# GpSimd's low parts wait for VectorE's: a scheduling hint becomes a dependency in an attention and channel-mixing kernel

## The chip, the cores and the metric

The kernel runs on one NeuronCore of a Trainium2 chip. The metric is the device time of one launch in microseconds. A core has five engines that run their own instruction queues in order and wait for one another by semaphores: TensorE (PE, with its weight loads shown apart as PEld), VectorE (DVE), ScalarE (ACT), GpSimd (POOL) and SyncE (SP), which here only issues DMA transfers.

## The reference

Eight batches, eight heads, 576 tokens, head size 64. First a windowed attention with a linear bias per head, then a mixing block on the attention's output:

```
scores = (q @ k^T) / sqrt(64) + slope[h] * -|i - j|, masked to 0 <= i - j < 128
x      = softmax(scores) @ v                    # [B, 576, 512], heads side by side
theta  = x @ w_theta
y      = w_tok_r @ (x * cos(theta)) + w_tok_i @ (x * sin(theta))
u      = x + y
out    = u + max(u @ w_ch, 0)
```

All inputs and outputs are float32.

## The kernel before

Products that need float32 accuracy are made of two parts. An operand is rounded to a high part, and the rest, operand minus high part, is its low part; a product is high x high + high x low + low x high. ACT makes the high parts (`qh`, `kh`, `vh`, `u_hi`, `z_hi`), and DVE or GpSimd the low parts: `ql` (L311) and `vl` (L331) on DVE, `kl` (L315) and `u_lo` (L573) on GpSimd, `z_lo` (L463) on either.

The work goes batch by batch. A batch of attention has four **pair steps**, g = 0 to 3, each for two heads; here g = 0 is the first step of a batch. In a step (`attend`) PE transposes the probabilities of the current pair (`flip`, into `t_ps`; ACT and DVE copy them out as the two parts of `pt`, L410 and L411), computes the scores of the next pair in three lots (the first into an `mm` bank, the others into `s_ps`; DVE adds the bias and takes the minimum at L395, ACT exponentiates at L398 into `last` and `s_sb`), and multiplies probabilities by values (`values`, into `acc`); DVE divides by the row sums (`finish`, L446 to L449, into `x_sb`). Between these pieces PE does the token mixing of the batch before (`mix`, products of `wtk` and `z`); at its end `u` is formed (DVE, L569), rounded (ACT, `u_hi`, L571) and its low part collected in a list, `lows`, that the step emits at its end. Then comes the **turn**: `x` is transposed, theta, cosine and sine are computed and `z` is made for the next batch's token mixing, with the channel mixing (`channels`, the products with `wch`) of the batch before in between.

Operands are prepared ahead. `prepare`, called in the middle of a step behind the first head's division, splits the q and k of one pair (`split_pair`: `qh`, `ql`, `kh`, `kl`) and then issues the loads of the next one: three transfers into `qr`, one into `kr` (L211 to L215), on SP's queue, which also carries the value loads (`vb`) and the outputs. `qr` and `kr` are single buffers: the next load waits until `qh` and `ql`, or `kh` and `kl`, have been made. The pair that is split in step g has its scores computed in step g + 1.

A scheduler lays down each engine's queue from the program's dependencies, from priorities and from hints. PE's order is pinned to the program's. A block under `tc.issue_after(ins)` puts an ordering edge, without a semaphore, from each instruction of the block that stands on the engine of `ins` to `ins`; an instruction of another engine gets none by it. The hints around `kl` and around `lows` name a DVE instruction (`ql`, or the second head's `vl`), while `kl` and `u_lo` are GpSimd's.

Of the kernel before, what the change touches and what calls it, by code (L numbers as in the profile page):

```python
# [11 lines left out]
F32 = mybir.dt.float32  # L12
# [6 lines left out]
ALU = mybir.AluOpType  # L19
# [27 lines left out]
def attn_moe_kernel(ctx: ExitStack, tc: tile.TileContext, qt, kt, vx, wth, wtok, wch, band, out):  # L47
    nc = tc.nc
# [19 lines left out]
    pinned, lows = [], []  # L68

    def mm(*args, **kw):  # L70
        ins = nc.tensor.matmul(*args, **kw)  # L71
        if pinned:
            tc.keep_in_program_order(ins)

    def flipped(*args):
        ins = nc.tensor.transpose(*args)  # L76
        if pinned:
            tc.keep_in_program_order(ins)
# [153 lines left out]
    def measure(g):  # L232

        vb = group_v[g]
        peak = peaks[g % 2]
        most = peak[:, :GROUP]
        nc.vector.tensor_reduce(out=most, in_=vb[:, :, :, :64], axis=mybir.AxisListType.XY, op=ALU.max,
                                apply_absolute_value=True)  # L240
        nc.vector.tensor_scalar(out=most, in0=most, scalar1=2.0 ** -100, scalar2=None, op0=ALU.max)
        group_v[g] = vb, peak
# [13 lines left out]
    def spread_to(diag, n, part):  # L256
        w_ps = ps_m.tile([128, 512], F32, name="mm")
        mm(w_ps[:, :n], ones.broadcast_to([128, 128]), diag, start=True, stop=True)
        scale = rings["scale" + part].take()
        power(scale, w_ps[:, :n], VEXP)  # L260
        return scale
# [12 lines left out]
    def spread_first(g):  # L274
        vb, peak = group_v[g]
        group_v[g] = vb, spread_from(peak, GROUP, "")

    def spread_scales(g):
        vb, diag = group_v[g]
        scale = spread_to(diag, GROUP, "")  # L280
        group_v[g] = vb, scale
        if g % 2:
            c = rings["scale"].at + (g // 2 - 1) % 2 * 2 * GROUP
            batch_scale(g // 2, fixed[:, c:c + 2 * GROUP])
# [19 lines left out]
    def split_pair(p, raw):  # L304

        qr, kr = raw
        qh, ql = (qk.tile([128, S + 64], F32R, name=name) for name in ("qh", "ql"))
        kh, kl = (qk.tile([128, S], F32R, name=name) for name in ("kh", "kl"))
        sc = scales[:, p % (H // 2):p % (H // 2) + 1]
        nc.scalar.activation(qh, qr, AF.Copy, scale=sc)  # L310
        low = nc.vector.scalar_tensor_tensor(out=ql, in0=qr, scalar=sc, in1=qh.bitcast(F32), op0=ALU.mult,  # L311
                                             op1=ALU.subtract)
        nc.scalar.copy(kh, kr)  # L313
        with tc.issue_after(low.ins) if pinned else nullcontext():
            nc.gpsimd.tensor_tensor(out=kl, in0=kr, in1=kh.bitcast(F32), op=ALU.subtract)  # L315
        return (qh, kh), (ql, kh), (qh, kl)

    def split_values(n):
# [27 lines left out]
    class Pair:  # L346
# [12 lines left out]
        def scores(self, tiles, behind=None):  # L359

            last = len(self.terms) - 1
            if tiles == (0,):
                _, _, k0, kn, _ = TILES[0]
                ps = ps_m.tile([128, 512], F32, name="mm")
                for j, (qm, km) in enumerate(self.terms):
                    mm(ps[:, :kn], qm[:, 512:], km[:, k0:k0 + kn], start=(j == 0), stop=(j == last))
                whole = lasts[self.p % len(lasts)]
                self.weigh(0, 0, whole[:, :kn], ps[:, :kn], bands[:, 512:], behind)
                self.sc[0, 0] = whole
                return  # L370
# [175 lines left out]
    def mix(st):  # L546

        xtf, z_hi, z_lo = st["xtf"], st["z_hi"], st["z_lo"]
        u_hi = big.tile([128, 4, S], F32R, name="u_hi")
        u_lo = big.tile([128, 4, S], F32R, name="u_lo")  # L550
        st.update(u_hi=u_hi, u_lo=u_lo)
        banks = {}
        seq = (8, 0, 4, 1, 5, 2, 6, 3, 7)

        def part(g, ks):
            hf, m = divmod(g, 4)
            cs = slice(hf * HALF, hf * HALF + HALF)
            if g not in banks:
                banks[g] = ps_m.tile([128, 512], F32, name="mm")
            y_ps = banks[g]  # L560
            for k in ks:
                c = seq[k]
                for n, (z, w) in enumerate(((z_hi, wtk_hi), (z_hi, wtk_lo), (z_lo, wtk_hi))):
                    mm(y_ps[:, :HALF], z[:, c, m * 128:m * 128 + 128], w[:, c, cs],
                       start=(k == 0 and n == 0), stop=(k == 8 and n == 2))
                if k < 8:
                    yield
            if ks[-1] == 8:
                nc.vector.scalar_tensor_tensor(out=xtf[:, m, cs], in0=y_ps[:, :HALF], scalar=st["back"],  # L569
                                               in1=xtf[:, m, cs], op0=ALU.mult, op1=ALU.add)  # L570
                nc.scalar.copy(u_hi[:, m, cs], xtf[:, m, cs])  # L571
                def low(m=m, cs=cs):
                    nc.gpsimd.tensor_tensor(out=u_lo[:, m, cs], in0=xtf[:, m, cs], in1=u_hi[:, m, cs].bitcast(F32),  # L573
                                            op=ALU.subtract)

                if st["b"] + 1 < B:
                    lows.append(low)
                else:
                    low()
                yield  # L580

        begun = 2 if st["b"] + 1 < B else 3
        for ks in (range(7), range(7, 9)):
            for g in range(begun):
                yield from part(g, ks)
        for g in range(begun, 8):
            yield from part(g, range(9))
# [28 lines left out]
    def prepare(p):  # L616

        if 0 <= p - 1 < pairs and p - 1 not in parts:
            parts[p - 1] = split_pair(p - 1, raw.pop(p - 1))
        if p < pairs and p not in raw:  # L620
            raw[p] = load_pair(p)

    def step(stream, k=1):
        for _ in range(k):
            next(stream, None)

    def attend(b, x_sb, mixing, chans, first, behind):

        for g in range(H // 2):
            p = b * H // 2 + g  # L630
            pair = first.pop(0)
            one, two = pair.heads
            new = None
            if p + DEPTH < pairs:
                new = Pair(p + DEPTH)
                first.append(new)
            measured = p // 2 + 1 if p % 2 == 0 and p + 2 < pairs else None
            scaled = p // 2 + 1 if p % 2 and p + 1 < pairs else None

            def scores(tiles):  # L640
                if new is not None:
                    new.scores(tiles, behind)

            steps = STEPS[min(g, 2)]
            pair.flip(0)
            pair.flip(2)
            step(mixing, steps[0])
            scores(SCORES[0])
            scores(SCORES[1])
            step(mixing, steps[1])  # L650
            pair.flip(1)
            pair.flip(3)
            step(mixing, steps[2])
            if scaled:
                with tc.high_priority(FINISH):
                    spread_first(scaled)
            one.values()
            with tc.high_priority(FINISH):
                done = one.finish(x_sb)
            scores(SCORES[2])  # L660
            if scaled:
                with tc.high_priority(FINISH):
                    spread_scales(scaled)
            with tc.issue_after(done.ins):
                if new is not None:
                    new.heads[0].ready()
                prepare(p + DEPTH + 2)
            step(mixing, steps[3])
            if g >= 2:
                step(chans)  # L670
            two.values()
            with tc.high_priority(FINISH):
                done = two.finish(x_sb)
            if new is not None:
                with tc.issue_after(done.ins):
                    done = new.heads[1].ready()
                    with tc.issue_after(done.ins):
                        for low in lows:
                            low()
                    if measured:  # L680
                        measure(measured)
            else:
                for low in lows:
                    low()
            lows.clear()
# [142 lines left out]
```

## Time and profile before

| | us |
|---|---|
| median of three runs | 732.91 (732.55 to 734.18) |
| profiled execution | 731.11, span 729.2 |
| busy: PE / DVE / ACT / POOL | 678.5 / 556.5 / 500.2 / 155.9 |
| `kl` L315, x32, busy, mean of one | 55.4, 1.73 |
| `u_lo` L573, x64, busy, mean of one | 50.6, 0.80 |

The busy times overlap, and each is counted over the whole span. Times in the profile's rows count from the start of the span. A row of the timeline gives start, duration, engine, line, operation, tiles (written, then read), shapes and, in brackets, how long the engine had been idle before and what ended that. The first 125 us or so are the start, in which weights are unpacked and the first batch's attention is computed; from there to about 640 us the same batch of four pair steps and a turn repeats, and the rest is the last batch's mixing.

### The profile page before, as it was taken

What the parts mean: (1) busy time and instruction counts of PE and PEld (TensorE: products, weight loads), DVE (VectorE), ACT (ScalarE), POOL (GpSimd) and SP (SyncE); (2) the same over time, 40 slices, a digit from 0 to 9 for tenths busy, and PEclk for the clock granted to TensorE, in tenths of its full rate; (3) what the DMA queues carried; (4) which work ended last, traced back from release to release, by engine and by line L of the source; (5) the groups of instructions that cost most, each with busy time, mean ns of one, the idle gap of its engine ahead of it and who ended that gap; (6) DMA issues with size and microseconds to landing.
All of it is one profiled execution on the core that took longest, in us unless ns stands there. A gap on an engine that the chain in (4) does not pass through costs nothing.

```text
span 729.2 us, 16045 instructions
## 1 busy us (share of the span) xinstructions
PE 678.5 (93%) x6219; PEld 578.7 (79%) x6221; DVE 556.5 (76%) x1528; ACT 500.2 (69%) x988; POOL 155.9 (21%) x200
## 2 busy tenths in 40 slices
PE   3889887999999999899999999899989999899998
PEld 2558765889878888788877898789878898789787
DVE  6988956887688967987688967987788967974722
ACT  4888467676966678666966678666966678654810
POOL 2211302321212302321212302321212301210220
PEclk9885588999999999999999999999999999999999
DMA  9556110232012310232012310232012310000001
GB/s 306 162 180 203 43 40 1 71 82 88 25 36 77 101 52 18 71 105 68 26 33 75 97 56 18 79 99 71 24 41 65 101 50 18 18 10 33 26 9 58
DMA packets 32620, 49.86 MB, mean 68 GB/s; under 512 B 5664, under 2 KB 22048, under 8 KB 32544
## 3 DMA queue, kind: packets, MB, share of 16 engines
q1 hardware_dynamic: 32544, 48.84, 21.9%
q8 instruction: 49, 0.80, 0.4%
q14 instruction: 27, 0.22, 0.1%
HBM read 39.39 MB, written 9.44 MB: 67 GB/s over the span
## 4 chain that ended last, share of the span: by engine, by line
PE 44%; DVE 25%; ACT 23%; issue 3%; DMA 3%; SPq 1%; POOL 0%; ACTq 0%; DVEq 0%; POOLq 0%
PE mm L71 28%; PE acc L71 6%; PE t_ps L76 5%; PE s_ps L71 4%; DVE pt L411 4%; ACT g L511 3%; ACT z_hi L462 3%; ACT g L510 3%; DVE ql L311 2%; ACT xtf L484 2%; DVE s_sb L395 2%; DVE g L515 2%; ACT x_hi L482 2%; DVE f L515 2%; ACT s_sb L398 1%
## 5 line engine op out<-in xcount | busy, mean ns | idle before, releaser
L71 PE MATMUL mm<-wtk_hi,z_lo 128*128 128x288 f16 x576 | 165.3, 287 | 5.6 <-DVE z_lo L463 5.0
L71 PE MATMUL mm<-wtk_hi,z_hi 128*128 128x288 f16 x576 | 165.7, 288 | 3.9 <-ACT z_hi L462 3.9
L71 PE MATMUL mm<-wtk_lo,z_hi 128*128 128x288 f16 x576 | 165.2, 287 | 0.0
L398 ACT ACTIVATE s_sb<-s_sb,fixed 128x256 f32<-128x256 f32 (+1 forms) x256 | 105.0, 472 | 50.4 <-DVE fixed L395 50.3
L71 PEld LDWEIGHTS <-z_hi 128*128 128x128 f16 x1152 | 109.1, 99 | 33.5 <-ACT z_hi L462 4.4
L573 POOL TENSOR_TENSOR u_lo<-xtf,u_hi 128x288 fp32r<-128x288 f32 x64 | 50.6, 797 | 293.1 <-ACT u_hi L571 277.6
L411 DVE SCALAR_TENSOR_TENSOR pt<-t_ps,pt 128x512 f16<-128x512 f32 x112 | 75.5, 686 | 37.3 <-ACT pt L410 36.9
L395 DVE CUSTOM_DVE_ANT_0 s_sb<-s_ps,bands 128x256 f32<-128x256 f32 (+1 forms) x256 | 85.5, 383 | 1.2 <-PE s_ps L71 1.2
L71 PEld LDWEIGHTS <-z_lo 128*128 128x128 f16 x576 | 56.4, 98 | 24.2 <-DVE z_lo L463 9.2
L76 PE MATMUL t_ps<-fixed,s_sb 128*128 128x128 f32 x448 | 66.0, 282 | 10.1 <-DVE pt L411 5.6
L315 POOL TENSOR_TENSOR kl<-kr,kh 128x576 fp32r<-128x576 f32 x32 | 55.4, 1731 | 63.6 <-ACT kh L313 63.6
L76 PEld LDWEIGHTS t_ps<-fixed,s_sb 128*128 128x128 f32 x448 | 51.9, 145 | 16.9 <-DVE pt L411 6.8
L410 ACT ACTIVATE pt<-t_ps 128x512 f16<-128x512 f32 x112 | 62.1, 580 | 4.1 <-PE t_ps L76 4.1
L571 ACT CAST u_hi<-xtf 128x288 fp32r<-128x288 f32 x64 | 27.1, 425 | 43.1 <-DVE xtf L569 43.1
L71 PE MATMUL acc<-vh,pt 128*128 128x65 f16 x1008 | 55.6, 194 | 0.0
L71 PEld LDWEIGHTS <-pt 128*128 128x128 f16 x1512 | 52.6, 98 | 2.7
L463 POOL TENSOR_TENSOR z_lo<-g,z_hi 128x512 f16<-128x512 f32 x16 | 19.2, 1198 | 160.4 <-ACT z_hi L462 160.4
L71 PE MATMUL acc<-vl,pt 128*128 128x64 f16 x504 | 52.1, 193 | 0.0
L71 PE MATMUL s_ps<-kh,qh 64*128 64x256 f32 (+1 forms) x256 | 44.2, 342 | 7.4 <-DVE fixed L395 7.3
L71 PE MATMUL mm<-wth_hi,x_hi 128*128 128x512 f32 x160 | 47.7, 421 | 3.2 <-ACT x_hi L482 1.7
L71 PE MATMUL mm<-u_hi,wch_hi 128*128 128x288 f32 x256 | 47.2, 306 | 0.0
L569 DVE SCALAR_TENSOR_TENSOR xtf<-mm,fixed,xtf 128x288 f32<-128x288 f32 x64 | 32.2, 512 | 18.7 <-PE mm L71 18.6
(141 smaller groups left out, 1540.9 us busy)
## 6 DMA issues: line engine op xcount, KB each, us to landing
vb<-in_vx_dram SPq DMA_DIRECT2D x16, 650.0 KB, 5.3
kr<-in_kt_dram SPq DMA_DIRECT2D x32, 288.0 KB, 3.2
out_dram<-xtf SPq DMA_DIRECT2D x64, 144.0 KB, 1.8
qr<-in_qt_dram SPq DMA_DIRECT2D x32, 144.0 KB, 2.7
qr<-in_qt_dram SPq DMA_DIRECT2D x32, 128.0 KB, 2.7
xtf<-in_wtok_dram SPq DMA_DIRECT2D x4, 576.0 KB, 4.6
u_hi<-in_wtok_dram SPq DMA_DIRECT2D x3, 576.0 KB, 4.6
u_lo<-in_wtok_dram SPq DMA_DIRECT2D x2, 576.0 KB, 5.9
```

The costliest lines, as they stand in the source:

```text
L71: ins = nc.tensor.matmul(*args, **kw)
L76: ins = nc.tensor.transpose(*args)
L315: nc.gpsimd.tensor_tensor(out=kl, in0=kr, in1=kh.bitcast(F32), op=ALU.subtract)
L395: nc.vector.tensor_tensor_reduce(out=sb, in0=ps, in1=bias, scale=2.0 ** -(2 * self.p % H + 1), scalar=3.0e38, op0=ALU.add, op1=ALU.min, ac ...
L398: self.exp = nc.scalar.activation(sb, sb, AF.Exp, bias=least, scale=-1.0)
L410: nc.scalar.activation(pt[:, 0], t_ps, AF.Copy, scale=2.0 ** PEXP)
L411: nc.vector.scalar_tensor_tensor(out=pt[:, 1], in0=t_ps, scalar=2.0 ** PEXP, in1=pt[:, 0], op0=ALU.mult, op1=ALU.subtract)
L462: st["turned"] = nc.scalar.copy(z_hi[:, c, :], z)
L515: nc.vector.scalar_tensor_tensor(out=z, in0=x_sb[:, i, :], scalar=zs[:, c:c + 1], in1=z, op0=ALU.mult, op1=ALU.mult)
L569: nc.vector.scalar_tensor_tensor(out=xtf[:, m, cs], in0=y_ps[:, :HALF], scalar=st["back"], in1=xtf[:, m, cs], op0=ALU.mult, op1=ALU.add)
L571: nc.scalar.copy(u_hi[:, m, cs], xtf[:, m, cs])
L573: nc.gpsimd.tensor_tensor(out=u_lo[:, m, cs], in0=xtf[:, m, cs], in1=u_hi[:, m, cs].bitcast(F32), op=ALU.subtract)
```

## The change

`kl` is made to wait, by a semaphore, for `ql` of the same pair, and each collected `u_lo` for the second head's `vl` of the step (`new.heads[1].ready()` returns it). A helper adds the dependency; the hints go. `kl` before the pinned part, and `u_lo` of the last batch, stay as they were.

```diff
+    def after(what, done):
+        tc.add_manual_dep(what.ins, done.ins.name, mybir.DependencyInfo(mybir.DependencyClass.Sync,
+                                                                         mybir.DependencyReason.DATA))
...
         nc.scalar.copy(kh, kr)
-        with tc.issue_after(low.ins) if pinned else nullcontext():
-            nc.gpsimd.tensor_tensor(out=kl, in0=kr, in1=kh.bitcast(F32), op=ALU.subtract)
+        rest = nc.gpsimd.tensor_tensor(out=kl, in0=kr, in1=kh.bitcast(F32), op=ALU.subtract)
+        if pinned:
+            after(rest, low)
...
                 def low(m=m, cs=cs):
-                    nc.gpsimd.tensor_tensor(out=u_lo[:, m, cs], in0=xtf[:, m, cs], in1=u_hi[:, m, cs].bitcast(F32),
-                                            op=ALU.subtract)
+                    return nc.gpsimd.tensor_tensor(out=u_lo[:, m, cs], in0=xtf[:, m, cs],
+                                                   in1=u_hi[:, m, cs].bitcast(F32), op=ALU.subtract)
...
                 with tc.issue_after(done.ins):
                     done = new.heads[1].ready()
-                    with tc.issue_after(done.ins):
-                        for low in lows:
-                            low()
+                    for low in lows:
+                        after(low(), done)
```

The scheduler then lays the queues down anew. The orders of PE and DVE stay the same, row by row. GpSimd's queue in the first two pair steps of a batch (the one whose `ql` stands at 212.76 us in the profile) was this before. Numbers behind a tile's name tell buffers apart: `kl_2821` belongs to the pair whose `qh` is `qh_2818`, and `kl_2581` to the pair ahead of it; in brackets stand the engines or DMA queues whose semaphores are waited for.

```order
L573 TENSOR_TENSOR u_lo_2406<-xtf_2120,u_hi_2405 128x288 [waits Activation_49,Pool_49]
L573 TENSOR_TENSOR u_lo_2406<-xtf_2120,u_hi_2405 128x288 [waits Activation_49]
L330 MEMSET vh_2573 128x5 [waits PE_49]
L315 TENSOR_TENSOR kl_2821<-kr_2589,kh_2820 128x576 [waits DMAHW5_49,PE_49,Activation_49]
L330 MEMSET vh_2631 128x5 [waits PE_49,Pool_49]
L573 TENSOR_TENSOR u_lo_2406<-xtf_2120,u_hi_2405 128x288 [waits Activation_49]
L330 MEMSET vh_2813 128x5 [waits PE_49,Pool_49]
L573 TENSOR_TENSOR u_lo_2406<-xtf_2120,u_hi_2405 128x288 [waits Activation_49]
L315 TENSOR_TENSOR kl_3047<-kr_2829,kh_3046 128x576 [waits DMAHW0_49,PE_49,Activation_49]
```

And now (its line numbers are those of the changed kernel, four or five higher):

```order
L335 MEMSET vh_2573 128x5 [waits PE_49,Pool_49]
L318 TENSOR_TENSOR kl_2581<-kr_2054,kh_2580 128x576 [waits DMAHW4_49,DVE_49]
L335 MEMSET vh_2631 128x5 [waits PE_49,Pool_49]
L578 TENSOR_TENSOR u_lo_2406<-xtf_2120,u_hi_2405 128x288 [waits DVE_49,Pool_49]
L578 TENSOR_TENSOR u_lo_2406<-xtf_2120,u_hi_2405 128x288 [waits Activation_49]
L335 MEMSET vh_2813 128x5 [waits PE_49,Activation_49,Pool_49]
L318 TENSOR_TENSOR kl_2821<-kr_2589,kh_2820 128x576 [waits DMAHW7_49,DVE_49,Activation_49]
```

Each `kl` stands one pair step later, with a wait for DVE, and two `u_lo` stand together at the end of each step, the first of them with a wait for DVE. ACT's queue changes with it, from the first head's `vh` of that step to the exponentials of the next scores. Before:

```order
L329 ACTIVATE vh_2573<-vb_1387,fixed_103 128x5x64 [waits PE_49]
L313 CAST kh_2820<-kr_2589 128x576 [waits DMAHW5_49,PE_49]
L398 ACTIVATE s_sb512_2551<-s_sb512_2551,fixed_103 128x256 [waits DVE_49]
...
L410 ACTIVATE pt_2655<-t_ps_2650 128x512 [waits PE_49,Activation_49]
L310 ACTIVATE qh_2818<-qr_126,fixed_103 128x640 [waits DMAHW7_49,DMAHW6_49,DMAHW5_49]
L398 ACTIVATE last1_105<-last1_105,fixed_103 128x192 [waits DVE_49]
```

Now:

```order
L334 ACTIVATE vh_2573<-vb_1387,fixed_103 128x5x64 [waits PE_49]
L403 ACTIVATE s_sb512_2551<-s_sb512_2551,fixed_103 128x256 [waits DVE_49]
...
L415 ACTIVATE pt_2655<-t_ps_2650 128x512 [waits PE_49,Activation_49]
L314 ACTIVATE qh_2818<-qr_126,fixed_103 128x640 [waits DMAHW6_49,DMAHW5_49,DMAHW4_49]
L317 CAST kh_2820<-kr_2589 128x576 [waits DMAHW7_49]
L403 ACTIVATE last1_105<-last1_105,fixed_103 128x192 [waits DVE_49]
```

`kh` moved from ahead of one set of exponentials to ahead of the next, behind its own pair's `qh`. On SP's queue the places stay; the `kr` load behind each three `qr` loads is now that of the same pair as these, where it was that of the pair after it.

## The prediction

> **What bounds the kernel now.** I read the page's busy shares first, then the list of waits for TensorE (PE), and then the timeline of one batch, engine by engine. The page gives the bound and the list of waits tells who ends PE's idle time (total us, times, longest).
>
> ```profile
> PE 678.5 (93%) x6219; PEld 578.7 (79%) x6221; DVE 556.5 (76%) x1528; ACT 500.2 (69%) x988; POOL 155.9 (21%) x200
> PE s_ps L71 <- DVE fixed L395: 7.3, 8, 1.7
> PE t_ps L76 <- DVE pt L411: 5.6, 8, 0.8
> PE t_ps L76 <- DVE peak L241: 2.2, 7, 0.3
> ```
>
> PE is busy 93% of the span; GpSimd (POOL) only 21%. So GpSimd's own work cannot matter directly: it matters if somebody waits for it or is held up by it. In the three rows VectorE (DVE) is what PE waits for, 15.1 us in all. I looked for the place in the timeline where DVE is late, and it is the first pair step (g = 0) of a batch. Here are DVE, then POOL, then PE in the batch that begins its pairs at about 203 us (columns: start us, duration us, engine, line, tiles, and in brackets the idle time before it and who ended it).
>
> ```profile
> 211.72 1.12 DVE L331 SCALAR_TENSOR_TENSOR vl<-vb,fixed,vh 128x320 f16<-128x320 f32 x1
> 212.76 2.03 DVE L311 SCALAR_TENSOR_TENSOR ql<-qr,fixed,qh 128x640 fp32r<-128x640 f32 x1
> ...
> 216.97 0.54 DVE L331 SCALAR_TENSOR_TENSOR vl<-vb,fixed,vh 128x320 f16<-128x320 f32 x1
> ...
> 218.82 0.68 DVE L411 SCALAR_TENSOR_TENSOR pt<-t_ps,pt 128x512 f16<-128x512 f32 x1
> ...
> 219.69 0.68 DVE L411 SCALAR_TENSOR_TENSOR pt<-t_ps,pt 128x512 f16<-128x512 f32 x1
> ...
> 621.83 2.02 DVE L311 SCALAR_TENSOR_TENSOR ql<-qr,fixed,qh 128x640 fp32r<-128x640 f32 x1
> ```
>
> ```profile
> L331 DVE SCALAR_TENSOR_TENSOR vl<-vb,fixed,vh x56: 538/543/1123, 88.4 to 651.0; 128x320 f16<-128x320 f32 x56
> L311 DVE SCALAR_TENSOR_TENSOR ql<-qr,fixed,qh x32: 841/877/2030, 7.7 to 634.6; 128x640 fp32r<-128x640 f32 x32
> 210.94 1.55 POOL L573 TENSOR_TENSOR u_lo<-xtf,u_hi 128x288 fp32r<-128x288 f32 x2 [12.81 <-ACT u_hi L571]
> 212.49 1.62 POOL L315 TENSOR_TENSOR kl<-kr,kh 128x576 fp32r<-128x576 f32 x1
> ```
>
> `vl` takes 0.54 us as a rule and 1.12 here, `ql` 0.88 as a rule (median 877 ns) and 2.03 here. GpSimd's `u_lo` pair runs to 212.49 and its `kl` to 214.11: `ql` ends 0.68 us after `kl` does, about its own length. The two DVE instructions are stretched by 0.58 and 1.15 us, together **1.73 us**, exactly while a GpSimd TENSOR_TENSOR is under way. It happens in six batches, the first at 212.76 and the last at 621.83 (2.02 us). PE in the same stretch:
>
> ```profile
> 215.21 0.27 PE L71 MATMUL mm<-kl,qh 128*128 128x192 f32 x1
> 216.22 0.33 PE L71 MATMUL s_ps<-kh,qh 64*128 64x128 f32 x2 [0.74 <-DVE fixed L395]
> 219.56 0.66 PE L76 MATMUL t_ps<-fixed,s_sb 128*128 128x128 f32 x4 [0.81 <-DVE pt L411]
> 220.52 0.63 PE L76 MATMUL t_ps<-fixed,s_sb 128*128 128x128 f32 x4 [0.31 <-DVE peak L241]
> ```
>
> PE then idles 0.74 + 0.81 + 0.31 = **1.86 us**, each time for DVE, and the DVE rows between (score reductions, `x_sb`, `vl`, the peak reduction, `pt`) follow each other without a break. So the 1.73 us lie on the path, 6 x 1.86 = 11.2 us of PE idle time at most.
>
> **The change part by part.** DVE's and PE's orders are the same in both kernels. On GpSimd, `kl` of a pair moves from one pair step ahead of its `ql` to just behind it, and the two `u_lo` of a step to behind the second head's `vl`. So at g = 0 nothing of GpSimd's low parts runs beside `vl` and `ql`: 1.73 us of DVE time come back, and DVE, which has no break until `pt` at 219.69, is 1.73 us earlier from there on.
>
> Does anybody wait for the late `kl`? `ql` would start at about 212.2 and end at 213.06, `kl` start right behind it, and the nearest row of a `kl` with no DVE partner is
>
> ```profile
> 251.39 1.51 POOL L315 TENSOR_TENSOR kl<-kr,kh 128x576 fp32r<-128x576 f32 x1 [1.34 <-ACT kh L313]
> L315 POOL TENSOR_TENSOR kl<-kr,kh x25: 1503/1819/1984, 133.0 to 621.6; 128x576 fp32r<-128x576 f32 x25
> ```
>
> so it ends at about 214.65, and PE's first use is at 215.21: 0.56 us to spare; even with the longest `kl` (1984 ns) it would end at 215.12. Behind `kl` on GpSimd stand only the ones-column memset and the two `u_lo`, whose readers (channel mixing) come two steps later. No cost there.
>
> The part that costs is ScalarE (ACT). `kh` moves from a place where ACT waited for PE anyway to right behind `qh`, ahead of the exponentials of the next scores. And `kr` is one buffer: its load, behind the `qr` loads on SP's queue as before, now brings the pair that is wanted next. It used to be issued at 216.70 for the `kh` at 225.11, 8.4 us ahead; now it lands just as `qh` is done. SP's queue, the landing time of `kr` between 128 and 645 us, and ACT:
>
> ```profile
> 216.70 0.53 SPq L215 DMA_DIRECT2D kr<-in_kt_dram  x1
> DMA to landing us min/median/max: 2.9/3.2/4.7
> 218.44 0.83 ACT L310 ACTIVATE qh<-qr,fixed 128x640 fp32r<-128x640 f32 x1
> 219.81 0.46 ACT L398 ACTIVATE last<-last,fixed 128x192 f32<-128x192 f32 x1 [0.55 <-DVE fixed L395]
> 220.69 1.09 ACT L398 ACTIVATE s_sb<-s_sb,fixed 128x128 f32<-128x128 f32 x3 [0.42 <-DVE fixed L395]
> ...
> 222.56 0.58 ACT L410 ACTIVATE pt<-t_ps 128x512 f16<-128x512 f32 x1
> ...
> 225.11 0.67 ACT L313 CAST kh<-kr 128x576 fp32r<-128x576 f32 x1 [0.36 <-PE s_ps L71]
> ```
>
> Everything here 1.73 us earlier: `kr` issued at 214.97 (`kl` is done at 214.65, so SP doesn't wait for it), landed at 217.9 to 218.2 by 2.9 to 3.2 us; `qh` from 216.71 to 217.54; `kh` from the landing, 0.67 us, to 218.6 to 218.9; then `last` (its 0.55 us of idle time takes up most of that), and `s_sb` 0.37 us behind `last`: 218.9 to 219.3, where 220.69 - 1.73 = 218.96 would be the ideal. So 0 to 0.35 us are given back, I take 0.18, because `pt` (222.56) and with it the value matmuls hang on these exponentials. Gain at g = 0: 1.73 - 0.18 = 1.55 us, of 1.86 us of PE idle time; six times, **9.3 us**.
>
> The same `kh` costs a little at the other steps. First g = 1 into g = 2, where `kr` is issued at 228.33:
>
> ```profile
> 228.33 0.54 SPq L215 DMA_DIRECT2D kr<-in_kt_dram  x1
> 230.95 0.58 ACT L410 ACTIVATE pt<-t_ps 128x512 f16<-128x512 f32 x1
> 232.50 1.49 ACT L398 ACTIVATE s_sb<-s_sb,fixed 128x128 f32<-128x128 f32 x4 [0.62 <-DVE fixed L395]
> 336.27 0.53 SPq L215 DMA_DIRECT2D kr<-in_kt_dram  x1
> 338.76 0.55 ACT L329 ACTIVATE vh<-vb,fixed 128x320 f16<-128x320 f32 x1
> 339.38 0.37 ACT L477 CAST x_hi<-t_ps 128x256 fp32r<-128x256 f32 x1
> ...
> 341.39 0.58 ACT L482 CAST x_hi<-t_ps 128x512 fp32r<-128x512 f32 x1 [0.40 <-PE t_ps L76]
> ```
>
> It lands at 231.5, as `pt` ends (231.53); `kh` to 232.2, `last` to 232.6, `s_sb` at 232.5: nothing, up to 0.5 us where the load lands later; 0.1 us in seven batches, **-0.7 us**. At the end of g = 3 `kh` comes between `vh` and the turn's first `x_hi`: landed at 339.5, done at 340.2, `x_hi` 0.7 us late, which the wait before 341.39 covers but for about 0.1 us, six times: **-0.6 us**. The turn is a chain from ACT to DVE and back, so without that cover it would be 0.7 each. In the first pinned batch DVE lost nothing (its `vl` and `ql` are of the usual length), but `kh` is late there as well:
>
> ```profile
> 135.88 0.52 SPq L215 DMA_DIRECT2D kr<-in_kt_dram  x1
> 139.57 0.69 ACT L398 ACTIVATE s_sb<-s_sb,fixed 128x128 f32<-128x128 f32 x2 [0.42 <-DVE fixed L395]
> ```
>
> landing 139.1, `kh` to 139.7, `s_sb` at 140.1 behind `last`: **-0.5 us**. One landing of 4.7 us, 1.5 over the median, with half of it covered: **-0.7 us**.
>
> One more partner for `kl`. In the program's start a small tensor_scalar took 1.04 us beside a GpSimd TENSOR_TENSOR, against 0.17 in the pair steps:
>
> ```profile
> 86.40 1.27 POOL L183 TENSOR_TENSOR wch_lo<-u_hi,wch_hi 128x512 fp32r<-128x512 f32 x1 [3.35 <-ACT wch_hi L182]
> 86.72 1.04 DVE L129 TENSOR_SCALAR fixed<-fixed 128x4 int32<-128x4 int32 x1
> 227.78 0.17 DVE L129 TENSOR_SCALAR fixed<-fixed 128x4 int32<-128x4 int32 x1
> ...
> 231.56 0.69 DVE L411 SCALAR_TENSOR_TENSOR pt<-t_ps,pt 128x512 f16<-128x512 f32 x1 [0.37 <-ACT pt L410]
> ```
>
> At g = 1 `ql` ends at 226.42, the new `kl` at about 228.0, and L129 stands at 227.78: 0.2 us of waiting, which DVE's 0.37 us of idle time before the `pt` at 231.56 takes up; I cost it at nothing, 0.2 us a batch without that cover. [...]
>
> Sum: 9.3 - 0.7 - 0.6 - 0.5 - 0.7 = **6.8 us**. The profiled execution took 731.1 us (span 729.2), so 724.3 by its own time; the median of the runs is 732.9, 1.8 us above it, and there 6.8 us less is **726.1 us**.
>
> **The rivals.** (1) *The whole idle time of PE comes back*: `kr` always lands before ACT gets to it, and DVE is never the last. 6 x 1.86 = 11.2 us, 721.7 us. For it: `last` has 0.55 us of idle time before it; against it: the landing at 2.9 to 3.2 us leaves ACT no slack at all. (2) *Nothing is gained*: ACT behind `kh` takes DVE's place as the one that PE waits for. If `kr` lands x us later than in these rows, g = 0 gains 1.55 - x and the step into g = 2 and the turn lose 0.1 + x each: 1.35 - 3x per batch, nothing at x = 0.45, a landing of 3.65 us. For it: the maximum of 4.7; against it: the median of 3.2, and the load stands at the same place behind the same `qr` loads. Time 732.9. (3) *Slower*: the same chain where SP itself stands still. L215 now waits for GpSimd's `kl`; if `kl` ends later than the three `qr` issues (0.32 us to spare at g = 0), `kr` and the `vb` and output transfers behind it go out late. At x = 0.7, `kl` at 1.98 us in place of 1.51 and semaphore steps on top, it is 1.35 - 2.1 = -0.75 us per batch, with the 1.2 us of the first batch and the late landing about 5.7 us: 738.6. It decides from x = 0.45 on. Against it: nothing that could stretch `kl` on DVE stands within 1.5 us behind `ql`. (4) *The change doesn't do what it says*, because the order was already kept: excluded by the rows at 210.94 and 212.49, where it wasn't.
>
> **How the numbers follow.** Forecast 0.71, rival 1 0.12, rival 2 0.10, rival 3 0.07. A difference of 0.2% is 1.5 us, about what a measurement here can tell from none. Forecast and rival 1 are faster, 0.83; rival 2 is the same, 0.10; rival 3 slower, 0.07. The range goes from rival 1 (721.7, so 722.0) to just short of rival 2 (732.0), since a landing time between the rows' 3.2 and 3.65 gives every value between; what is left out is rival 3, half of rival 2 and the edge of rival 1. The forecast's own range is 723.5 to 729.
>
> **What would show it.** Right: no `vl` or `ql` above 0.9 us after 128 us; `kl` right behind `ql` at 1.4 to 1.6 us; PE's three waits at g = 0 gone or below 0.4 us in all; ACT idle for the `kr` load before `kh`, by up to 0.8 us. Wrong: `s_ps` or `t_ps` still waiting for DVE there (the stall was not GpSimd's), PE waiting for `kl`, or a wait of PE for `pt` at the value matmuls that is as long as what was gained (rival 2).

## The result, and the profile after

The changed kernel takes **725.79 us** (median of four runs, 724.59 to 727.66) against 732.73 us (four runs, 732.33 to 734.18) before: a ratio of 0.9907, with a 95% interval of 0.9889 to 0.9926. The forecast was 726.1. The profiled execution took 726.36 us, its span 724.6.

The page's busy times, and from the list of waits who ends PE's idle time (total us, times, longest). In the changed file the lines lie four or five further down: `ql` is L315, `kl` L318, `vl` L336, `u_lo` L578, `kh` L317, the `kr` load L219.

```profile
PE 679.8 (94%) x6221; PEld 579.0 (80%) x6221; DVE 546.4 (75%) x1528; ACT 497.6 (69%) x988; POOL 147.4 (20%) x200
PE s_ps L71 <- DVE fixed L400: 3.7, 4, 1.7
PE t_ps L80 <- DVE peak L245: 2.2, 7, 0.3
PE t_ps L80 <- DVE pt L416: 1.8, 3, 0.9
PE acc L71 <- DVE pt L416: 1.0, 2, 0.5
```

DVE is busy 10.1 us less (556.5 before), with the same instructions. Two of the three waits of PE shrank, from 7.3 to 3.7 us (what is left of it stands in the program's start, before 56 us) and from 5.6 to 1.8 us; the third, for the peak reduction, is the 2.2 us that it was; a new one, of the value matmuls for `pt`, has 1.0 us. DVE's 10.1 us are `ql` (7.0 us less in all) and `vl` (5.0 us less), while all other instructions together take 1.9 us more. The lengths of `vl`, `ql` and `kl` between 128 and 645 us (minimum, median, maximum in ns):

```profile
L336 DVE SCALAR_TENSOR_TENSOR vl<-vb,fixed,vh x53: 541/544/553, 134.7 to 641.8; 128x320 f16<-128x320 f32 x53
L315 DVE SCALAR_TENSOR_TENSOR ql<-qr,fixed,qh x26: 874/877/880, 135.2 to 630.0; 128x640 fp32r<-128x640 f32 x26
L318 POOL TENSOR_TENSOR kl<-kr,kh x26: 1412/1424/1439, 136.2 to 631.1; 128x576 fp32r<-128x576 f32 x26
```

No `vl` and no `ql` is stretched any more (1123 and 2030 ns at most before), and `kl` itself is shorter (median 1819 before). The prediction counted six stretched `vl`. The profile of before has six more, of 0.73 us in place of 0.54, in the last step of each batch beside a `u_lo` (the first at 173.40 us); they are gone too, and what they cost cannot be told, because the step that they stand in differs by up to 0.65 us between two executions of the kernel before. The place that the prediction worked on, the first pair step of the batch whose pairs begin at about 203 us, now reads, in the timeline of DVE and POOL and then of PE:

```profile
214.07 0.55 DVE L336 SCALAR_TENSOR_TENSOR vl<-vb,fixed,vh 128x320 f16<-128x320 f32 x1
214.54 0.88 DVE L315 SCALAR_TENSOR_TENSOR ql<-qr,fixed,qh 128x640 fp32r<-128x640 f32 x1
215.50 1.42 POOL L318 TENSOR_TENSOR kl<-kr,kh 128x576 fp32r<-128x576 f32 x1 [2.67 <-DVE ql L315]
...
217.56 0.27 PE L71 MATMUL mm<-kl,qh 128*128 128x192 f32 x1
217.76 0.33 PE L71 MATMUL s_ps<-kh,qh 64*128 64x128 f32 x2
220.18 0.66 PE L80 MATMUL t_ps<-fixed,s_sb 128*128 128x128 f32 x4
221.15 0.63 PE L80 MATMUL t_ps<-fixed,s_sb 128*128 128x128 f32 x4 [0.31 <-DVE peak L245]
```

`kl` starts 0.08 us behind `ql`'s end and is done at 216.92, 0.64 us before PE needs it. The idle times of 0.74 and 0.81 us are gone; the 0.31 us for the peak reduction stay. The step from one first score matmul to the next, before and after (length, PE busy, granted clock, share and rate of the DMA):

```profile
214.91:229.56 14.65, 12.79 (x154) 1.00 0.37 108
```

```profile
217.26:230.35 13.09, 12.69 (x154) 1.00 0.39 109
```

1.56 us shorter, at the same full clock. What it costs stands on ACT, and SP, at the same place:

```profile
217.34 0.52 SPq L219 DMA_DIRECT2D kr<-in_kt_dram  x1
...
219.09 0.83 ACT L314 ACTIVATE qh<-qr,fixed 128x640 fp32r<-128x640 f32 x1 [0.18 <-DMA qr<-in_qt_dram]
220.87 0.67 ACT L317 CAST kh<-kr 128x576 fp32r<-128x576 f32 x1 [0.95 <-DMA kr<-in_kt_dram]
221.45 0.45 ACT L403 ACTIVATE last<-last,fixed 128x192 f32<-128x192 f32 x1
221.80 1.08 ACT L403 ACTIVATE s_sb<-s_sb,fixed 128x128 f32<-128x128 f32 x3
```

and in ACT's list of waits between 128 and 645 us:

```profile
ACT kh L317 <- DMA kr<-in_kt_dram: 8.7, 13, 1.5
```

ACT waits for the `kr` load, 0.95 us here and 8.7 us in 13 of the 25 steps. Before, the list of the whole span has 14.1 us ahead of `kh` for PE and 0.6 for a load.

### The profile page after: what moved, and what is told of

Its sections match the earlier page's. It is cut to its first block, busy times and chain, and to the rows that moved or that the text cites. A ratio compares the mean times of both kernels' runs of the same rounds, so it can differ in the third digit from the quotient of the medians.

```text
span 724.6 us, 16027 instructions
## 1 busy us (share of the span) xinstructions
PE 679.8 (94%) x6221; PEld 579.0 (80%) x6221; DVE 546.4 (75%) x1528; ACT 497.6 (69%) x988; POOL 147.4 (20%) x200
## 4 chain that ended last, share of the span: by engine, by line
PE 38%; ACT 26%; DVE 22%; DMA 6%; issue 3%; SPq 3%; POOL 0%; ACTq 0%; DVEq 0%; POOLq 0%
PE mm L71 25%; PE acc L71 5%; PE t_ps L80 4%; DVE pt L416 4%; PE s_ps L71 4%; ACT g L516 3%; DMA kr<-in_kt_dram 3%; ACT z_hi L467 3%; ACT s_sb L403 3%; ACT g L515 3%; ACT xtf L489 2%; DMA qr<-in_qt_dram 2%; DVE g L520 2%; DVE ql L315 2%; ACT pt L415 2%
## 5 line engine op out<-in xcount | busy, mean ns | idle before, releaser
L318 POOL TENSOR_TENSOR kl<-kr,kh 128x576 fp32r<-128x576 f32 x32 | 46.5, 1454 | 105.2 <-DVE ql L315 55.4
L578 POOL TENSOR_TENSOR u_lo<-xtf,u_hi 128x288 fp32r<-128x288 f32 x64 | 50.0, 800 | 85.1 <-DVE vl L336 51.4
L335 POOL MEMSET vh<- 128x5 f16 x56 | 6.8, 121 | 215.5 <-PE acc L71 215.5
```

The source lines that it names most:

```text
L318: rest = nc.gpsimd.tensor_tensor(out=kl, in0=kr, in1=kh.bitcast(F32), op=ALU.subtract)
L578: return nc.gpsimd.tensor_tensor(out=u_lo[:, m, cs], in0=xtf[:, m, cs], in1=u_hi[:, m, cs].bitcast(F32), op=ALU.subtract)
```

## The experiments

All times are medians beside runs of the kernel before on the same chip (732.61 us for the first four, 733.06 for the others).

### Only the low part of k waits

```diff
 # the changed kernel, but:
-                    for low in lows:
-                        after(low(), done)
+                    with tc.issue_after(done.ins):
+                        for low in lows:
+                            low()
```

> Only the low part of k gets the wait; the two low parts of u of a step keep the mere hint. ScalarE, VectorE, TensorE and SyncE run in the order of the changed kernel, GpSimd alone has the low parts of u back ahead of the values' low part. Theory (a GpSimd TENSOR_TENSOR and a two-input VectorE instruction shut each other out, and the shut-out time lies on the path): at g = 0 vl is about 1.1 us again and ql 0.88, so of the 1.73 us of each batch 0.58 are lost again, six times 3.5 us: 725.8 + 3.5 = 729.3 us. Rival (the stretch of vl is taken up by VectorE's idle time, only ql's is on the path): 725.8 us with vl at 1.1. Rival (the gain came from the new places of kh and kr, the contention is beside the path): 725.8 us too, and then the kernel with only u's wait gains nothing.

**728.43 us**, ratio 0.9947 (0.9929 to 0.9965). The same batch, DVE and POOL:

```profile
214.49 1.54 POOL L578 TENSOR_TENSOR u_lo<-xtf,u_hi 128x288 fp32r<-128x288 f32 x2 [12.81 <-ACT u_hi L576]
215.27 1.11 DVE L336 SCALAR_TENSOR_TENSOR vl<-vb,fixed,vh 128x320 f16<-128x320 f32 x1
216.31 0.87 DVE L315 SCALAR_TENSOR_TENSOR ql<-qr,fixed,qh 128x640 fp32r<-128x640 f32 x1
```

`vl` is stretched again, `ql` not, and 2.6 us of the gain are lost (3.5 expected): the stretch of `vl` is on the path, and both rivals fall.

### Only the low parts of u wait

```diff
 # the changed kernel, but:
-        rest = nc.gpsimd.tensor_tensor(out=kl, in0=kr, in1=kh.bitcast(F32), op=ALU.subtract)
-        if pinned:
-            after(rest, low)
+        with tc.issue_after(low.ins) if pinned else nullcontext():
+            nc.gpsimd.tensor_tensor(out=kl, in0=kr, in1=kh.bitcast(F32), op=ALU.subtract)
```

> Only the low parts of u get the wait; kl keeps the hint. ScalarE, VectorE, TensorE and SyncE run in the order of the kernel before, so kh is computed one step ahead and waits for no load. vl is 0.54 everywhere. kh ends at about the moment at which ql can begin (212.25 and 212.20 us in the trace of before), so by the theory ql has one of two lengths: 0.9 us where it begins first (then the whole stall is gone and nothing is given back: 722 to 724 us), or about 2.3 us where kl begins first (then 1.4 to 1.5 of 1.73 us stay: 730 to 732 us). [...] Rival (the gain came from kh and kr): 732.7 us, as before.

**721.89 us**, ratio 0.9860 (0.9837 to 0.9883): half of the change gains more than the whole. No other kernel here that computes everything has a lower median, though the one with the `kr` load a step ahead, 722.49 us, cannot be told from it. DVE and POOL in the timeline:

```profile
214.57 0.55 DVE L335 SCALAR_TENSOR_TENSOR vl<-vb,fixed,vh 128x320 f16<-128x320 f32 x1
215.04 0.88 DVE L315 SCALAR_TENSOR_TENSOR ql<-qr,fixed,qh 128x640 fp32r<-128x640 f32 x1
215.18 2.02 POOL L319 TENSOR_TENSOR kl<-kr,kh 128x576 fp32r<-128x576 f32 x1 [1.85 <-ACT kh L317]
```

The lengths of `ql` and `kl` between 128 and 645 us, and behind them the step on PE, by the windows:

```profile
L315 DVE SCALAR_TENSOR_TENSOR ql<-qr,fixed,qh x26: 873/876/881, 135.7 to 625.4; 128x640 fp32r<-128x640 f32 x26
L319 POOL TENSOR_TENSOR kl<-kr,kh x25: 1504/1973/2025, 135.9 to 613.9; 128x576 fp32r<-128x576 f32 x25
```

```profile
217.77:230.70 12.93, 12.62 (x154) 1.00 0.37 112
```

`kl` still runs beside `ql`, but it begins 0.14 us after it, in this batch as in the other five. Now `kl` is the stretched one (2.02 us; 1.42 alone), and nobody waits for it. Without the `u_lo` pair in front, `vl` is done early enough for `ql` to come first. `ql` has one of the two lengths (0.88 us here, 2.03 where `kl` began first), not one between. And since `kl` keeps its hint, the scheduler leaves `kh` where it was before, a step ahead of its need, with no load to wait for.

### kr a step ahead

```diff
 # the changed kernel, with two buffers for kr in turn; ahead of the old kr load:
+        if p > 6:
+            while len(krs) < 2:
+                kr = ld.tile([128, S], F32, name="kr2" if next_kr[0] % 2 else "kr")
...
+                    go = nc.sync.dma_start(out=kr, in_=kt[bn, hn:hn + 2].rearrange("h d s -> (h d) s"))
...
+            return qr, krs.pop(0)
```

> The changed kernel with two buffers for kr, and the kr load behind the qr loads at the same place of the queue brings the pair after the next. kr is then there a step before it is wanted; VectorE's, TensorE's and GpSimd's order is that of the changed kernel, and kh stands on ScalarE where it stood before the change. Theory (what was given back is kh waiting for its late load): ScalarE's 9.3 us of waiting for kr are gone, no vl or ql is stretched, and at g = 0 only 0.3 us of TensorE idle time for the peak reduction stays: 6 x (1.86 - 0.31) = 9.3 us and a little for the late landings, 722.5 us (721 to 724). Rival (kh's late place cost nothing, the rest of the gain is lost elsewhere): 725.8 us.

**722.49 us**, ratio 0.9873 (0.9848 to 0.9898), as the theory had it. ACT's waits ahead of `kh` over the span:

```profile
ACT kh L332 <- POOL vh L350: 12.1, 6, 2.2
ACT kh L332 <- PE s_ps L71: 3.2, 11, 0.4
ACT kh L332 <- DMA kr<-in_kt_dram: 1.1, 2, 0.6
```

The wait for the load is down from 9.3 to 1.1 us over the whole span, and the median time by 3.3 us; the two ratios' intervals touch, so the size of that is uncertain. The scheduler also puts `kh` back to where it stood on ACT before the change, so this run takes away both the wait for `kr` and the late place of `kh`: together they are what the changed kernel gives back. The intervals of this kernel and of the one in which only u waits overlap: with the load ahead, `kl`'s wait costs nothing that shows, and gains nothing either.

### kr later still

```diff
 # the changed kernel, ahead of each kr load:
+            after(nc.sync.dma_start(out=spare, in_=qt[b, h + 1, :, 512:]), ql_done[-1])
```

> The changed kernel with one more small load (64x64, read by nobody) ahead of each kr load, which makes kr, and the loads behind it, about 0.55 us later; the order on all other engines is that of the changed kernel. Theory (kh waits for kr, and its lateness goes through the exponentials to TensorE in three of the four steps of a batch): up to 3 x 0.55 = 1.65 us a batch, ten in all with the first batch; part of it is covered, so 731 us (729 to 736). Rival (ScalarE has the slack): 725.8 us, within 1 us.

**733.14 us**, ratio 1.0025 (1.0002 to 1.0048): the whole gain is gone. From the lists of waits of ACT and PE over the span:

```profile
ACT kh L321 <- DMA kr<-in_kt_dram: 21.5, 24, 2.4
PE mm L71 <- DVE x_hi L487: 4.7, 7, 1.7
PE acc L71 <- DVE pt L420: 3.6, 8, 0.5
```

No `vl` or `ql` is stretched here, yet PE waits at the turn (`x_hi`, 1.2 us in all in the changed kernel) and for `pt` at the value matmuls (1.0 us). The `kr` load goes out 1.34 us behind the last `qr` load in place of 0.70 (221.31 and 219.97, against 217.34 and 216.64), so 0.64 us later; 25 loads, and 7.35 us: 0.29 us for each. The extra load could have delayed other loads as well; but ACT waits 20.0 us for `qr` between 128 and 645 us, against 19.0 in the changed kernel, and nobody waits for `vb`, so nearly all of what grew is the wait for `kr`. This is the prediction's second rival, made to happen.

### GpSimd busy, but reading nothing

```diff
 # the kernel before, in the batches (low parts of k and u left out):
-            nc.gpsimd.tensor_tensor(out=kl, in0=kr, in1=kh.bitcast(F32), op=ALU.subtract)
+                for _ in range(3):
+                    low_k.append(nc.gpsimd.memset(kl.bitcast(F32), 0.0))
+                    after(low_k[-1], high)       # waits for kh, as kl did
...
+                        for _ in range(2):
+                            after(nc.gpsimd.memset(u_lo[:, m, cs].bitcast(F32), 0.0), high)
```

The next `kr` load is made to wait for the last fill, as it waited for `kl`.

> The kernel before, with all instructions of the other engines in its order, but in the batches that are written out GpSimd fills kl with zeros three times (128x576, some 0.6 us each) and each u_lo twice in place of subtracting: the low parts of k and u are left out, GpSimd is as busy as before at the same places, but reads nothing. Theory (it is GpSimd's reading of SBUF beside a VectorE instruction with two SBUF inputs that stretches it): vl 0.54 and ql 0.88 us in all batches though a GpSimd fill runs beside them, and the time of the kernel with only u's wait, 722 us (721 to 723.5). [...]

**721.57 us**, ratio 0.9846 (0.9826 to 0.9865). DVE and POOL at g = 0, and all `ql` and all fills of `kl` between 128 and 645 us:

```profile
212.22 0.55 DVE L344 SCALAR_TENSOR_TENSOR vl<-vb,fixed,vh 128x320 f16<-128x320 f32 x1
212.69 0.88 DVE L319 SCALAR_TENSOR_TENSOR ql<-qr,fixed,qh 128x640 fp32r<-128x640 f32 x1
211.41 1.01 POOL L588 MEMSET u_lo<- 128x288 f32 x3 [12.78 <-ACT u_hi L584]
212.81 1.86 POOL L325 MEMSET kl<- 128x576 f32 x3
```

```profile
L319 DVE SCALAR_TENSOR_TENSOR ql<-qr,fixed,qh x26: 874/877/881, 133.3 to 624.0; 128x640 fp32r<-128x640 f32 x26
L325 POOL MEMSET kl<- x75: 577/579/585, 133.5 to 613.8; 128x576 f32 x75
```

The fills run beside `vl` and `ql`, and neither is longer than alone. For `ql` that alone tells little, since it begins 0.12 us ahead of the first fill of `kl`, and such a lead saved it beside a subtraction too. Two other rows decide. The third `u_lo` fill is under way when `vl` begins at 212.22 (the three end at 212.42), and `vl` still takes 0.55 us, where keeping it out to the fill's end would have made it about 0.2 us longer. And no fill of `kl` is longer than 585 ns, whether `ql` runs beside it or not, where the subtraction that began 0.14 us behind `ql` took 2.02 us in place of 1.42. So GpSimd's being busy is not enough: `vl` takes 0.55 us behind a fill that began first, 1.12 behind a subtraction. The subtractions differ from the fills in that they read two tiles, and in that they subtract; an instruction that reads without subtracting was not tried.

### kl in two halves

```diff
 # the kernel before, in the batches:
+                for cs in (slice(0, HALF), slice(HALF, S)):
+                    nc.gpsimd.tensor_tensor(out=kl[:, cs], in0=kr[:, cs], in1=kh[:, cs].bitcast(F32), op=ALU.subtract)
```

> The kernel before, but kl is subtracted in two instructions of 288 columns (0.8 us each) in place of one of 576 (1.42 us when undisturbed), at the same place; the order elsewhere is that of before. Theory (one instruction keeps the other engine out to its own end, no longer): at g = 0 ql gets in between the two halves and takes about 1.4 us in place of 2.03, six times 0.6 us: 729 us (728 to 730), while the second half waits for ql. Rival (GpSimd's queued instructions together keep VectorE out): ql 2.1 to 2.2 us, 733 us. [...]

**728.09 us**, ratio 0.9940 (0.9920 to 0.9961). DVE and POOL at g = 0:

```profile
213.38 1.12 DVE L335 SCALAR_TENSOR_TENSOR vl<-vb,fixed,vh 128x320 f16<-128x320 f32 x1
214.16 2.34 POOL L317 TENSOR_TENSOR kl<-kr,kh 128x288 fp32r<-128x288 f32 x2
214.43 1.41 DVE L311 SCALAR_TENSOR_TENSOR ql<-qr,fixed,qh 128x640 fp32r<-128x640 f32 x1
```

`ql` takes 1.41 us in place of 2.03: it gets in between the halves, and the pair of halves takes 2.34 us in place of about 1.6. It ends at 215.84, 0.88 us (its length alone) behind 214.96, where a first half of 0.8 us (the shortest takes 793 ns) would end, and 0.66 us ahead of the end of the second at 216.50. So by this estimate the first half kept `ql` out to its own end, and the second, queued behind it, did not. A split and no wait at all gains 0.6 of the 1.15 us that `ql` was stretched by.

### Both kernels once more

> The kernel before once more, for a second profile of its start (0 to 122 us, the same order in all kernels). If the start's clock and loads differ from run to run, its first pair step after the turn begins at another time than the 121.80 us of the first profile, by up to 2.8 us as in the other kernels (123.10 to 124.57 us); if the changed kernels themselves start later, it is at 121.8 again.

> The changed kernel once more, for a second profile: the start as in the run of the kernel before beside it, and the gain of a first pair step of a batch again 1.3 to 1.7 us, the step after it giving back up to 0.7 us where kr lands later than 3.4 us. If the step that gained only 0.53 us in the first profile (the fifth batch, kr landed after 3.8 us) gains 1.3 us or more now, a single late landing was the cause and not the place in the program.

One execution each: **731.71** and **723.47 us**. The first score matmul behind the start stands in the timeline of the kernel before at

```profile
136.09 0.35 PE L71 MATMUL mm<-kh,qh 128*128 128x192 f32 x1
```

in that of the kernel before, executed again, at

```profile
137.17 0.35 PE L71 MATMUL mm<-kh,qh 128*128 128x192 f32 x1
```

and in those of the changed kernel, first and again, at

```profile
138.45 0.35 PE L71 MATMUL mm<-kh,qh 128*128 128x192 f32 x1
```

```profile
137.85 0.35 PE L71 MATMUL mm<-kh,qh 128*128 128x192 f32 x1
```

The same kernel reaches this point 1.1 us apart in two executions, and the ten profiled executions lie between 136.1 and 139.5 (the latest is that in which only k waits). So a difference between two profiled executions has 1 to 3 us of the start in it, which are not the change's. From this point on the steps can be compared one by one. In the table, for each execution, the first column adds up how much shorter the six steps are that begin at the first score matmul near 215, 297, 379, 460, 542 and 624 us (g = 0) than in the first profile of before, and the second column all other steps from 136 to 639 us; both from the starts of those matmuls in the timelines.

| kernel | the six steps at g = 0 | their sum, us | other steps, us |
|---|---|---|---|
| before again | +0.01, +0.02, -0.01, +0.01, 0.00, +0.03 | +0.1 | -0.5 |
| changed | -1.56, -1.71, -1.26, -0.53, -1.69, -1.72 | -8.5 | +1.4 |
| changed again | -1.71, -1.72, -0.78, -1.72, -1.62, -1.70 | -9.2 | -0.1 |
| only k waits | -1.16, -1.14, -0.49, -1.15, -1.17, -1.15 | -6.3 | +1.8 |
| only u waits | -1.72, -1.72, -1.73, -1.72, -1.73, -1.72 | -10.3 | -1.8 |
| kr a step ahead | -1.72, -1.70, -1.73, -1.72, -1.73, -1.71 | -10.3 | +1.1 |
| kr later still | -1.47, -1.36, -0.81, -0.13, -0.35, -1.60 | -5.7 | +8.5 |
| reading nothing | -1.72, -1.72, -1.73, -1.72, -1.73, -1.72 | -10.3 | -0.8 |
| kl in halves | -0.59, -0.61, -0.61, -0.59, -0.61, -0.60 | -3.6 | -1.3 |

Wherever no load is late, a step at g = 0 gains 1.72 us without `u_lo` and `kl` ahead of `vl` and `ql`, 1.15 where `vl` stays stretched (0.57 less) and 0.60 with the halves. What is left over in these six steps belongs to late loads. The worst one of the first profile of the changed kernel, at 460 us, SP, ACT and PE:

```profile
458.88 1.32 SPq L217 DMA_DIRECT2D qr<-in_qt_dram  x1
460.31 0.52 SPq L219 DMA_DIRECT2D kr<-in_kt_dram  x1
...
464.13 0.67 ACT L317 CAST kh<-kr 128x576 fp32r<-128x576 f32 x1 [1.52 <-DMA kr<-in_kt_dram]
...
467.41 0.24 PE L71 MATMUL acc<-vh,pt 128*128 128x65 f16 x2 [0.49 <-DVE pt L416]
```

and the same load and `kh` in the second profile of the changed kernel, where that step gained 1.72 us:

```profile
457.86 0.94 SPq L217 DMA_DIRECT2D qr<-in_qt_dram  x1
...
461.70 0.67 ACT L317 CAST kh<-kr 128x576 fp32r<-128x576 f32 x1 [0.37 <-DMA kr<-in_kt_dram]
```

In the first, the issue of the last `qr` load took 1.32 us in place of 0.59, `kr` went out late and landed 3.8 us after its issue; in the second the same issue took 0.94 us, and `kr` landed 2.8 us after its own. So that step's loss was one execution's late landing, as the expectation had it. But the place has a part: that issue was long both times, and in all ten profiled executions one `qr` issue near 400 us and one near 470 us took 1.0 to 1.8 us (1.32 and 1.46 in the first profile of before, 1.38 and 1.80 in that of the changed kernel).

Nor is it always `kr` that is late. At the third g = 0 every kernel with a late `kh` loses (the changed one in both profiles, the one in which only k waits, the one with `kr` later still), and there ACT in the first profile of the changed kernel reads

```profile
381.40 0.83 ACT L314 ACTIVATE qh<-qr,fixed 128x640 fp32r<-128x640 f32 x1 [1.56 <-DMA qr<-in_qt_dram]
382.14 0.66 ACT L317 CAST kh<-kr 128x576 fp32r<-128x576 f32 x1
```

`qr` is late, `kr` is there, and `kh`, now behind `qh`, holds up the exponentials. In the kernel in which only u waits, `qh` waits as long at the same place (1.51 us), but the exponentials follow it at once, and the step gains all of its 1.72 us.

## Why the prediction was right, point by point

**The stall and its size: right.** The prediction had 1.73 us of DVE time lying on the path in six batches, 10.4 us. The table has 1.72 us in each step with no late load, 10.3 us in three different kernels that remove the stall in three ways. That GpSimd's subtractions cause it, and not its mere work, is shown by the fills (`vl` 0.55 and `ql` 0.88 us beside them), that `ql` and `vl` count separately by the two half changes (0.57 of 1.72 us belong to `vl`, predicted 0.58).

**`kl` has 0.56 us to spare: right.** It was 0.64, and no row of PE's waits names `kl`. The row that the length was taken from was misread: the `kl` of 1.51 us at 251.39 did have a DVE partner, the `ql` from 250.74 to 251.62. Alone `kl` takes 1.42 us, which is where the further 0.08 us come from.

**`kh` behind its late load gives part of it back: right in the sum, wrong in the form.** The prediction took off 0.18 at each g = 0, 0.1 at each step into g = 2 and at each turn, 0.5 in the first pinned batch and 0.7 for one late landing, 3.6 us in all. The measured sum is 725.79 - 721.89 = 3.9 us, by the kernel without `kl`'s wait, or 3.3 us by the kernel with `kr` ahead. But where both loads land in time, a step gives back nothing: `kh` 0.37 us behind its load at 461.70 cost none of the 1.72 us. And where one lands late, that costs 0.5 to 1.2 us: at five steps of the first profile (0.5 and 1.2 us at the third and the fourth g = 0, 0.6 to 0.7 us at three steps into g = 2), at one of the second (0.9 us at the third g = 0). In the first profile it is `kr` at two of the five (`kh` at 313.47 and 464.13 waits 1.26 and 1.52 us for it) and `qr` at the others (`qh` at 381.40, 393.82 and 475.56 waits 1.3 to 1.6 us, `kh` behind it at most 0.1); in the second it is `qr` (2.01 us). The term that was mis-sized is thus the late landing: one, of `kr`, at 0.7 us in the prediction; five, about 3.6 us in all, in the first profile, and a late `qr` was not reckoned with at all. Of the constant terms, 2.9 us in all, little or nothing shows. That 3.6 us still came out close to the measured sum is luck. Part by part:

- at g = 0, predicted 1.1 us in all, measured 1.9 in the first profile and 1.1 in the second (10.34 less 8.47 and 9.24), nearly all in one or two steps;
- at the steps into g = 2, predicted 0.1 each: against before 0.6 to 0.7 at three steps in the first profile and nothing at the others, 0.2 at most in the second (the last of them differs by 0.7 us between the two profiles of before);
- at the turns, predicted 0.6 in all: 0.6 and 1.0 us more than in the kernel in which only u waits, but the kernel before differs there from itself by -0.5 to +0.7 in a single step, so this is not told from nothing;
- in the first pinned batch, predicted 0.5: nothing, its four steps from 136 us on differ by 0.03 us at most in both profiles.

**ACT idle ahead of `kh` by up to 0.8 us: not quite.** 0.67 us in the mean (8.7 us, 13 times), but 1.52 at most.

**PE's three waits of 0.74, 0.81 and 0.31 us at g = 0.** The first two went, the third stayed, as the sum (1.55 of 1.86) allowed for, though for another reason: it hangs on the peak reduction of DVE, not on the late `kh`. That a step is still shorter by 1.72, and not by 1.55 us, shows in PE's busy time, 12.79 before and 12.62 us in the kernel where only u waits: 0.17 us of the gain lie inside what the profile counts as busy.

**The small tensor_scalar beside `kl`.** It costs nothing, as taken, but it is stretched:

```profile
L133 DVE TENSOR_SCALAR fixed<-fixed x13: 157/273/280, 149.1 to 632.3; 128x4 int32<-128x4 int32 x13
```

Seven of these take 0.27 or 0.28 us beside the new `kl`, in place of 0.17, half of the 0.2 us of waiting that was worked out. The step at 458 us in the second profile has an `L133` of 0.28 us and gains all of its 1.72 us.

**The rivals.** The first (all of PE's idle time back, 721.7 us) is not what this change does, but it is what half of it does: 721.9 us with `u`'s wait alone. The second (a late `kr` eats the gain) is the right mechanism with too steep a slope: it had 3x a batch, or 0.75x a step; the kernel with the extra load lost 0.29 us a step for x = 0.64, that is about 0.45x, so ACT has some slack. The third (SP held up by a late `kl`) did not happen: `kl` was done at 216.92, the last `qr` load was issued until 217.23.

**`kl`'s wait: more than `ql` needs.** In the kernel where only u waits, `kl` runs beside `ql`, and a lead of 0.14 us is enough: `ql` takes 0.88 us, and `kl` the 2.02.

**What stays open.** Why one `kr` load lands after 2.8 and another after 4.7 us, and why issues are long near 400 and 470 us in every execution, is not settled. What the late loads cost at the other steps, the turns above all, is not told from the spread between executions.

## What to carry to other kernels

Where instructions of two engines stretch each other, look at which of them comes first and who waits for the other: here it was enough that `ql`, the one on the critical path, started 0.14 us ahead of `kl` (0.88 us in place of 2.03), and `kl` in two halves gave back 0.6 us of the stretch. A wait is not free even where its instruction has time to spare (0.64 us here): this one moved what depends on it, `kh` and the reuse of a single buffer, to a place where the loads are only just in time (8.7 us of waiting for `kr` in 13 steps); after adding one, look at what the scheduler moved and give that load a second buffer, or leave that wait out. When two profiled executions are compared, line them up at a point behind the part that varies from run to run, and take the steps from there.

## What the runs showed of the hardware that was not expected

- Which of `ql` and `kl` is stretched turns on a lead of 0.14 us: `ql` 0.88 and `kl` 2.02 us where `ql` begins that much ahead, `ql` 2.03 and `kl` 1.62 us where `kl` begins 0.27 us ahead.
- The stretch of `ql` ended with the first half of `kl`, not with both: between the two queued halves the waiting `ql` gets in (1.41 us).
- GpSimd fills (0.58 us each) beside the same `ql` leave it at 0.88 us, and take no longer themselves.
- An instruction of four elements a partition, `L133`, is stretched beside `kl` too, from 0.17 to 0.27 us.
- Issuing one load of `qr` took 1.0 to 1.8 us in place of 0.5 to 0.6 at two places, near 400 and near 470 us, in all ten profiled executions; the load behind it on the queue went out late by that (1.46 us from 472.59 and the next issue at 474.14 in the first profile of before, 1.80 from 471.42 and 473.31 in that of the changed kernel).
